# Mish as h·(1−2r): one multiply by h instead of two, a cap on exp(h), and a new instruction order

## The chip, the core and the metric

The kernel runs on one core of one Trainium2 chip. The metric is the device time of one execution in microseconds (us); lower is better. Three runs of the kernel before took 521.38, 521.48 and 521.93 us, a median of 521.48.

## The reference

Two stages follow each other. The first is a gated linear recurrence over 768 steps for 4 batches of 8 heads of width 48; the second is a feed-forward layer with the activation mish, over all 3072 tokens:

```python
f = 1.0 / (1.0 + np.exp(-f_logit))
for t in range(S):
    state = f[:, :, t, :, None] * state + np.einsum('bhd,bhe->bhde', k[:, :, t], v[:, :, t])
    y[:, :, t] = np.einsum('bhd,bhde->bhe', q[:, :, t], state)
...
h = x @ w_in                                   # 3072 x 384 times 384 x 2048
sp = np.where(h > 20.0, h, np.log1p(np.exp(np.minimum(h, 20.0))))
g = h * np.tanh(sp)
return (g @ w_out).astype(np.float32)          # 3072 x 2048 times 2048 x 384
```

With u = exp(h), tanh(log(1+u)) is n/(n+2) for n = u² + 2u, and that is also 1 − 2r for r = 1/((u+1)² + 1).

## The kernel before

**Recurrence.** The sequence is cut into 24 chunks of 128 steps (6 chunks times 4 batches). A chunk `n` goes through four steps, `attn0` to `attn3`. `load` and `prep` bring in `l`, `k`, `q`, `v` and scale `k` and `q` by decays: L386 caps the logits, L387 and L388 take exp and log, L391 (a matmul) or L396 (a scan) sums along the chunk, L403 and L404 take the exponentials, and L306 multiplies `k` and `q`. L427 forms the scores, L433 masks them into `a`. L452 transposes `k`, L455 copies it out, L470 forms the state update, L483 or L486 and L488 add it (`mid`, `tmp`), and L533 decays the state on GpSimd. L505 and L517 form the outputs; L543 to L550 split them into a high and a low part in `xt`, and L556 moves one quarter of `xt` by DMA to the place where the feed-forward wants it.

**Feed-forward.** Four chunks make a group of 512 tokens, and the hidden width is cut into 16 blocks of 128, so there are 6 × 16 = 96 units. For each unit L247 runs 9 matmuls into one of two PSUM tiles `h` (three slices of the model width, each as high·high, low·high and high·low products), `mish` turns `h` into `g`, then into `gh` (L264) and the rest `gl` (L265), and L270 runs 9 matmuls into three PSUM tiles `o`, two units behind (`LAG = 2`). A unit's L247 can only start when the mish of two units earlier has read its `h` for the last time, at L263. Weights come as 64-bit numbers and are split by `split_w` (L349 to L359) during the first 16 blocks.

**Mish before.** L257 and L258 on ScalarE give u with a cap at 10, L259 on VectorE gives n, L260 h·n, L261 and L262 on ScalarE 1/(n+2) as exp(−log(n+2)), L263 the product, L264 the high part, L265 on GpSimd the rest:

```python
("act", ..., lambda: nc.scalar.activation(u, h, AF.Relu, bias=hcap, scale=-1.0)),          # L257
("act", ..., lambda: nc.scalar.activation(u, u, AF.Exp, bias=hcap, scale=-1.0)),           # L258
("dve", ..., lambda: nc.vector.scalar_tensor_tensor(n, u, 2.0, u, ALU.add, ALU.mult)),     # L259
```

**Order.** All steps are collected in `Plan` with a cost each; `pack` lays them out on the engines, `SEEDS` names random changes of the ranking, and the kernel issues the instructions of every engine in the order of the planned starts. Each engine works through its own queue in that order. Until the first L270 the plan also puts filler matmuls (`idle`, L339, on a tile of zeros) where it expects the TensorE to have nothing to do. One filler in the program is two matmuls in the trace, as every matmul on plain f32.

Of the kernel before, what the change touches and what calls it, by code (L numbers as in the profile page):

```python
# [35 lines left out]
H_CAP = 10.0  # L36
# [11 lines left out]
]  # L48
NR = 3
LAG = 2  # L50

# [151 lines left out]
def recurrence_moe_kernel(  # L203
# [29 lines left out]
    two = ctile([P, 1], F32, "two")  # L233
    hcap = ctile([P, 1], F32, "hcap")
# [18 lines left out]
    def mish(h, n, g, gh, gl):  # L253

        u = n
        return (
            ("act", T_ACT(GT, True, 1), 0, lambda: nc.scalar.activation(u, h, AF.Relu, bias=hcap, scale=-1.0)),  # L257
            ("act", T_ACT(GT, False, 1), 0, lambda: nc.scalar.activation(u, u, AF.Exp, bias=hcap, scale=-1.0)),  # L258
            ("dve", T_DVE(GT), 1, lambda: nc.vector.scalar_tensor_tensor(n, u, 2.0, u, ALU.add, ALU.mult)),  # L259
            ("dve", T_DVE(GT), 0, lambda: nc.vector.tensor_tensor(g, h, n, ALU.mult)),  # L260
            ("act", T_ACT(GT, False, 1), 0, lambda: nc.scalar.activation(h, n, AF.Ln, bias=two)),  # L261
            ("act", T_ACT(GT, True), 0, lambda: nc.scalar.activation(h, h, AF.Exp, scale=-1.0)),  # L262
            ("dve", T_DVE(GT), 0, lambda: nc.vector.tensor_tensor(g, g, h, ALU.mult)),  # L263
            ("act", T_ACT(GT), 0, lambda: nc.scalar.activation(gh, g, AF.Copy)),  # L264
            ("pool", T_POOL(GT), 1, lambda: nc.gpsimd.tensor_tensor(gl, g, gh.bitcast(F32), ALU.subtract)),  # L265
        )
# [8 lines left out]
    with tc.tile_pool(name="work", bufs=1) as pool, tc.tile_pool(  # L275
# [33 lines left out]
        def consts():  # L309
# [6 lines left out]
            nc.gpsimd.memset(two, 2.0)  # L316
            nc.gpsimd.memset(hcap, H_CAP)
            nc.gpsimd.memset(ones, 1.0)

# [282 lines left out]
        def out_unit(u):  # L602
# [18 lines left out]
            if last:  # L621
                dst = halves[g] if j < NF - 1 else out[:, g * GT : (g + 1) * GT]
                for m in range(NK):
                    if part:
                        add("dve", T_DVE(GT), lambda m=m: nc.vector.tensor_tensor(ob_[m], o_[m], ob_[m], ALU.add),
# [190 lines left out]
```

## Time and profile before

| | |
|---|---|
| median of three runs | 521.48 us |
| span of the profiled execution, first to last instruction | 519.1 us |
| TensorE busy (matmul) | 505.9 us, 97% |
| ScalarE busy | 416.4 us, 80% |
| VectorE busy | 366.7 us, 71% |
| GpSimd busy | 156.1 us, 30% |
| first L247 starts | 45.29 us |
| last L270 group starts, 45 matmuls | 502.56 us |

The profiled execution has no time of its own beside its span; what lies around the span is taken as 521.48 − 519.1 = 2.4 us, the distance to the median. PE is the TensorE's matmuls, PEld its weight loads, ACT the ScalarE, DVE the VectorE, POOL the GpSimd, SP the queue that issues the DMAs. A busy PE is no proof of a PE at its best rate, because matmuls overlap and their ends are modelled; the distance between starts tells the rate.

### The profile page before, as it was taken

Reading aid. Unit: us, or ns where it says so; the run is one execution under the profiler, and the core shown is the slowest. Engines: PE = TensorE matmul, PEld = TensorE weight load, DVE = VectorE, ACT = ScalarE, POOL = GpSimd, SP = SyncE. Lnnn points to the kernel's source line nnn. Section 1 sums busy time; section 2 is a strip of 40 time slices with the busy share of each in tenths; the row PEclk is TensorE's granted clock in tenths of the full one; section 3 lists DMA queues with packets and bytes.
Section 4 is the critical chain, followed back from the end, with each engine's and each line's share of the span. In section 5 each row is a group of like instructions: output and inputs, shape, how many; then the busy total and the mean of one; then the engine's idle time right before and its main releaser. Section 6 shows DMA issues by size and latency. Waiting matters only on the chain.

```text
span 519.1 us, 12812 instructions
## 1 busy us (share of the span) xinstructions
PE 505.9 (97%) x5250; PEld 399.9 (77%) x5250; DVE 366.7 (71%) x592; ACT 416.4 (80%) x731; POOL 156.1 (30%) x134
## 2 busy tenths in 40 slices
PE   8799999999999999999999999999999999999995
PEld 6677777777787778778778778778787787878884
DVE  3679999999997876856767667665668564545451
ACT  6698988988999888888778788877778786777771
POOL 1142443333332223232233232323232221232322
PEclk9799999999999999999999999999999999999999
DMA  8977634524601533320213321130210000010001
GB/s 257 346 227 265 218 125 152 158 87 142 221 25 38 189 102 111 124 59 27 82 40 92 104 82 43 45 101 10 74 49 1 4 2 32 2 60 0 1 1 66
DMA packets 22625, 48.86 MB, mean 94 GB/s; under 512 B 2656, under 2 KB 3808, under 8 KB 22560
## 3 DMA queue, kind: packets, MB, share of 16 engines
q1 hardware_dynamic: 22560, 47.98, 28.2%
q8 instruction: 42, 0.69, 0.5%
q14 instruction: 23, 0.19, 0.1%
HBM read 39.32 MB, written 6.29 MB: 88 GB/s over the span
## 4 chain that ended last, share of the span: by engine, by line
PE 85%; DVE 5%; ACT 3%; DMA 2%; issue 2%; SPq 1%; POOL 0%; DVEq 0%; ACTq 0%
PE h L247 37%; PE o L270 36%; PE at L517 2%; PE at L505 2%; PE at L470 2%; PE at L427 2%; PE at L452 2%; DMA raw<-ww 1%; DMA l<-fl 1%; DVE wt L356 1%; SPq L368 1%; PE o L339 1%; DVE n L259 1%; DVE wt L354 1%; DVE g L263 1%
## 5 line engine op out<-in xcount | busy, mean ns | idle before, releaser
L265 POOL TENSOR_TENSOR gl<-g,gh 128x512 fp32r<-128x512 f32 x96 | 128.9, 1344 | 292.9 <-ACT gh L264 257.0
L247 PE MATMUL h<-xt,wh 128*128 128x512 f32 x576 | 185.0, 402 | 1.2 <-DVE g L263 1.2
L247 PEld LDWEIGHTS h<-xt,wh 128*128 128x128 f32 x576 | 105.2, 188 | 27.7 <-DVE g L263 2.9
L270 PE MATMUL o<-gh,wh 128*128 128x512 f32 x288 | 116.0, 403 | 0.0
L247 PE MATMUL h<-xt,wl 128*128 128x512 f32 x288 | 113.7, 395 | 0.0
L270 PE MATMUL o<-gh,wl 128*128 128x512 f32 x288 | 113.7, 395 | 0.0
L270 PE MATMUL o<-gl,wh 128*128 128x512 f32 x288 | 113.7, 395 | 0.0
L259 DVE SCALAR_TENSOR_TENSOR n<-n 128x512 f32<-128x512 f32 x96 | 67.9, 707 | 54.6 <-ACT n L258 54.2
L257 ACT ACTIVATE n<-h,hcap 128x512 f32<-128x512 f32 x96 | 65.7, 685 | 32.6 <-PE h L247 31.9
L263 DVE TENSOR_TENSOR g<-g,h 128x512 f32<-128x512 f32 x96 | 65.4, 682 | 36.8 <-ACT h L262 36.2
L261 ACT ACTIVATE h<-n,two 128x512 f32<-128x512 f32 x96 | 65.9, 686 | 18.6 <-DVE g L260 17.5
L264 ACT ACTIVATE gh<-g 128x512 fp32r<-128x512 f32 x96 | 60.1, 627 | 19.3 <-DVE g L263 14.1
L260 DVE TENSOR_TENSOR g<-h,n 128x512 f32<-128x512 f32 x96 | 66.2, 690 | 9.3 <-POOL gl L265 1.3
L258 ACT ACTIVATE n<-n,hcap 128x512 f32<-128x512 f32 x96 | 69.2, 721 | 2.3
L270 PEld LDWEIGHTS o<-gh,wh 128*128 128x128 f32 x288 | 54.0, 187 | 13.7 <-issue 0.3
L270 PEld LDWEIGHTS o<-gl,wh 128*128 128x128 f32 x288 | 54.0, 187 | 13.2
L247 PEld LDWEIGHTS h<-xt,wl 128*128 128x128 f32 x288 | 54.0, 187 | 13.2
L270 PEld LDWEIGHTS o<-gh,wl 128*128 128x128 f32 x288 | 54.1, 188 | 12.0
L262 ACT ACTIVATE h<-h 128x512 f32<-128x512 f32 x96 | 55.8, 582 | 1.7
L396 DVE TENSOR_TENSOR_SCAN cum<-go,l 128x512 f32<-128x512 f32 x20 | 26.9, 1343 | 0.9 <-ACT l L388 0.8
L433 DVE TENSOR_TENSOR a<-at,causal 128x256 f32<-128x256 f32 x44 | 17.6, 418 | 10.5 <-PE at L427 10.5
L533 POOL TENSOR_TENSOR state<-tmp,ends 128x256 f32<-128x256 f32 x20 | 16.0, 802 | 24.8 <-PE at L505 16.9
(103 smaller groups left out, 500.6 us busy)
## 6 DMA issues: line engine op xcount, KB each, us to landing
raw<-ww SPq DMA_DIRECT2D x16, 768.0 KB, 4.9
v<-vn SPq DMA_DIRECT2D x24, 256.0 KB, 3.7
k<-kk SPq DMA_DIRECT2D x23, 256.0 KB, 3.0
q<-qq SPq DMA_DIRECT2D x23, 256.0 KB, 3.7
l<-fl SPq DMA_DIRECT2D x20, 256.0 KB, 2.7
out<-ob SPq DMA_DIRECT2D x18, 256.0 KB, 2.9
xt<-xt SPq DMA_DIRECT2D x15, 128.0 KB, 2.1
half<-ob SPq DMA_DIRECT2D x6, 256.0 KB, 2.2
```

Source lines behind the costliest of these rows:

```text
L247: nc.tensor.matmul(h, w[:, j, a * P : (a + 1) * P], xt[:, x, a, :], start=(n == 0), stop=(n == 3 * NK - 1))
L257: ("act", T_ACT(GT, True, 1), 0, lambda: nc.scalar.activation(u, h, AF.Relu, bias=hcap, scale=-1.0)),
L258: ("act", T_ACT(GT, False, 1), 0, lambda: nc.scalar.activation(u, u, AF.Exp, bias=hcap, scale=-1.0)),
L259: ("dve", T_DVE(GT), 1, lambda: nc.vector.scalar_tensor_tensor(n, u, 2.0, u, ALU.add, ALU.mult)),
L260: ("dve", T_DVE(GT), 0, lambda: nc.vector.tensor_tensor(g, h, n, ALU.mult)),
L261: ("act", T_ACT(GT, False, 1), 0, lambda: nc.scalar.activation(h, n, AF.Ln, bias=two)),
L262: ("act", T_ACT(GT, True), 0, lambda: nc.scalar.activation(h, h, AF.Exp, scale=-1.0)),
L263: ("dve", T_DVE(GT), 0, lambda: nc.vector.tensor_tensor(g, g, h, ALU.mult)),
L264: ("act", T_ACT(GT), 0, lambda: nc.scalar.activation(gh, g, AF.Copy)),
L265: ("pool", T_POOL(GT), 1, lambda: nc.gpsimd.tensor_tensor(gl, g, gh.bitcast(F32), ALU.subtract)),
L270: nc.tensor.matmul(o, w[:, j, m * P : (m + 1) * P], x, start=(first and i == 0), stop=(last and i == 2))
L396: add("dve", 2 * T_DVE(w) - 70, lambda s=s, cum=cum: nc.vector.tensor_tensor_scan(cum.rearrange("p a c -> p (a c)"), go[:, s].rearrange("p ...
```

## The change

Mish is computed as −2·h·(r − ½) with r = 1/((u+1)² + 1), and the factor −2 is put into the copies that take `o` out of PSUM. There are eight operations instead of nine: exp on ScalarE straight from `h`, cap and +1 in one VectorE operation, a square on ScalarE, log and exp as before but written to `n` in SBUF, and one VectorE operation that subtracts ½ and multiplies by `h`. The cap is now exp(10) on u. The tile `half`, which holds ½, is made at the start by two small ScalarE operations; two memsets go. `SEEDS` is replaced by another list and the whole order is packed anew. Since lines move, L247 of before is L244 in the changed kernel, L257 and L258 become L258 (exp), L259 (cap and +1) and L255 (square); L261 to L265 keep their numbers and L260 is gone.

```diff
-H_CAP = 10.0
+U_CAP = 22026.46484375
 SEEDS = [
-    10000067, 10000086, ...
+    13000029, 13000046, ...
...
+        square = (
+            ("dve", T_DVE(GT), 1, lambda: nc.vector.tensor_tensor(n, n, n, ALU.mult)) if on_dve else
+            ("act", T_ACT(GT), 0, lambda: nc.scalar.activation(n, n, AF.Square))
+        )
         return (
-            ("act", T_ACT(GT, True, 1), 0, lambda: nc.scalar.activation(u, h, AF.Relu, bias=hcap, scale=-1.0)),
-            ("act", T_ACT(GT, False, 1), 0, lambda: nc.scalar.activation(u, u, AF.Exp, bias=hcap, scale=-1.0)),
-            ("dve", T_DVE(GT), 1, lambda: nc.vector.scalar_tensor_tensor(n, u, 2.0, u, ALU.add, ALU.mult)),
-            ("dve", T_DVE(GT), 0, lambda: nc.vector.tensor_tensor(g, h, n, ALU.mult)),
-            ("act", T_ACT(GT, False, 1), 0, lambda: nc.scalar.activation(h, n, AF.Ln, bias=two)),
-            ("act", T_ACT(GT, True), 0, lambda: nc.scalar.activation(h, h, AF.Exp, scale=-1.0)),
-            ("dve", T_DVE(GT), 0, lambda: nc.vector.tensor_tensor(g, g, h, ALU.mult)),
+            ("act", T_ACT(GT, True), 0, lambda: nc.scalar.activation(n, h, AF.Exp)),
+            ("dve", 70 + GT / 1.92, 1, lambda: nc.vector.tensor_scalar(n, n, U_CAP, 1.0, ALU.min, ALU.add)),
+            square,
+            ("act", T_ACT(GT, False, 1), 0, lambda: nc.scalar.activation(n, n, AF.Ln, bias=ones)),
+            ("act", T_ACT(GT), 0, lambda: nc.scalar.activation(n, n, AF.Exp, scale=-1.0)),
+            ("dve", T_DVE(GT), 0, lambda: nc.vector.scalar_tensor_tensor(g, n, half_, h, ALU.subtract, ALU.mult)),
             ("act", T_ACT(GT), 0, lambda: nc.scalar.activation(gh, g, AF.Copy)),
...
-            nc.gpsimd.memset(two, 2.0)
-            nc.gpsimd.memset(hcap, H_CAP)
             nc.gpsimd.memset(ones, 1.0)
+            nc.scalar.activation(half_, ones, AF.Ln, bias=ones)
+            nc.scalar.activation(half_, half_, AF.Exp, scale=-1.0)
...
-    nc.vector.tensor_tensor(ob_[m], o_[m], ob_[m], ALU.add)
+    nc.vector.scalar_tensor_tensor(ob_[m], o_[m], -2.0, ob_[m], ALU.mult, ALU.add)
-    nc.scalar.activation(ob_[m], o_[m], AF.Copy)
+    nc.scalar.activation(ob_[m], o_[m], AF.Copy, scale=-2.0)
-    nc.vector.tensor_copy(ob_[m], o_[m])
+    nc.vector.tensor_scalar(ob_[m], o_[m], -2.0, None, ALU.mult)
```

`SQ_DVE` is empty, so all 96 squares run on ScalarE. The three places at which the new order matters follow; a number behind a tile's name tells one buffer from another.

The TensorE where the feed-forward starts, in the kernel before: the transpose for the sixth chunk, three fillers, the first unit (`h_129`), then the update of the sixth chunk.

```order
L517 MATMUL at_127<-a_100,v_91 32x64
L452 MATMUL at_128<-ident,k_86 128x128 x4
L339 MATMUL o_133<-state_74 128x256 x3
L247 MATMUL h_129<-xt_107,wh 128x512 x2
L247 MATMUL h_129<-xt_107,wl 128x512
L247 MATMUL h_129<-xt_107,wh 128x512 x2
L247 MATMUL h_129<-xt_107,wl 128x512
L247 MATMUL h_129<-xt_107,wh 128x512 x2
L247 MATMUL h_129<-xt_107,wl 128x512
L470 MATMUL at_128<-v_92,kt_96 64x64 x2
```

The same place in the changed kernel:

```order
L517 MATMUL at_126<-a_99,v_90 32x64
L452 MATMUL at_127<-ident,k_85 128x128 x4
L244 MATMUL h_128<-xt_106,wh 128x512 x2
L244 MATMUL h_128<-xt_106,wl 128x512
L244 MATMUL h_128<-xt_106,wh 128x512 x2
L244 MATMUL h_128<-xt_106,wl 128x512
L244 MATMUL h_128<-xt_106,wh 128x512 x2
L244 MATMUL h_128<-xt_106,wl 128x512
L244 MATMUL h_129<-xt_106,wh 128x512 x2
L244 MATMUL h_129<-xt_106,wl 128x512
```

The three fillers ahead of the first unit are gone, and the second unit (`h_129`) follows the first with nothing in between. Over the whole program the TensorE has 21 fillers instead of 28: ahead of the first unit 18 instead of 25, and behind it three in each.

The TensorE a little later, in the kernel before: the last fillers, between the outputs of the sixth chunk and the third unit, which takes the `h` of the first.

```order
L517 MATMUL at_126<-a_101,v_92 32x64
L517 MATMUL at_127<-a_102,v_92 32x64
L339 MATMUL o_133<-state_74 128x256 x2
L247 MATMUL h_129<-xt_107,wh 128x512 x2
L247 MATMUL h_129<-xt_107,wl 128x512
```

In the changed kernel the last fillers stand behind the second unit, ahead of the update of the sixth chunk; its scores and then the third unit follow.

```order
L244 MATMUL h_129<-xt_106,wh 128x512 x2
L244 MATMUL h_129<-xt_106,wl 128x512
L339 MATMUL o_132<-state_73 128x256 x3
L470 MATMUL at_127<-v_91,kt_95 64x64 x2
L470 MATMUL at_126<-v_91,kt_95 64x64 x2
```

So in the changed kernel the third unit comes with less recurrence work ahead of it: the sixth chunk's outputs and the seventh's transpose, which lay between the second and the third unit, now come behind the third.

SP's queue where the first group's `xt` is moved, in the kernel before (`raw` is a block of weights, 768 KB):

```order
L556 DMA xt_107<-xt_107 32x2x384
L349 DMA raw_122<-ww 128x1536
L556 DMA xt_107<-xt_107 32x2x384 x2
L556 DMA xt_107<-xt_107 32x2x128 x3
L371 DMA v_90<-vn 128x512
```

And in the changed kernel:

```order
L368 DMA k_83<-kk 128x512
L368 DMA q_86<-qq 128x512
L556 DMA xt_106<-xt_106 32x2x384 x3
L556 DMA xt_106<-xt_106 32x2x128 x3
L349 DMA raw_121<-ww 128x1536
L371 DMA v_89<-vn 128x512
```

All six transfers of `xt` now go ahead of the block of weights instead of five behind it.

## Rows read from the trace of the kernel before

**Rows 1.** Busy time by 20 us stretches, two of them: bounds of the stretch, its length, then busy us and (instructions) of PE, PEld, DVE, ACT and POOL, the granted TensorE clock, the DMA engines' share, GB/s.

```profile
40.00:60.00 20.00, 19.03 (x310) 14.46 (x302) 20.00 (x33) 17.64 (x33) 6.16 (x5) 1.00 0.68 231
...
140.00:160.00 20.00, 20.00 (x87) 15.87 (x86) 18.03 (x27) 19.12 (x32) 6.08 (x5) 1.00 0.12 33
```

**Rows 2.** The chain of work that ended last, towards its end: start, length, what (the third row is the last group of matmuls).

```profile
456.36 4.20 PE h L247 x18
460.56 4.20 PE o L270 x18
...
502.56 10.52 PE o L270 x45
```

**Rows 3.** Waits of the TensorE in the whole span, those of the feed-forward: line <- what it waited for: us in total, times, longest.

```profile
PE h L247 <- DVE g L263: 1.2, 3, 0.6
```

**Rows 4.** The chain of work that ended last, from 16 to 30 us.

```profile
16.57 0.57 PE o L427 x23
17.14 2.01 issue
...
19.73 2.00 PE h L391 x8
...
23.91 0.85 PE o L339 x2
...
25.19 0.73 PE o L339 x2
25.93 0.89 PE at L391 x8
...
27.25 0.87 PE o L339 x4
...
28.75 1.06 PE o L339 x4
```

**Rows 5.** Busy time in one stretch of 1 us, columns as in rows 1.

```profile
24.00:25.00 1.00, 1.00 (x5) 0.82 (x5) 0.32 (x1) 0.64 (x2) 0.11 (x1) 0.50 0.65 141
```

**Rows 6.** The TensorE in order of time, the last correction matmul of the first group and the first unit: start, us, engine, line, operation, tiles, shapes, count; where there is a bracket, the idle time ahead of it and what ended it.

```profile
37.57 0.38 PE L546 MATMUL at<-xt,minus 128*128 128x256 f32 x1
...
45.29 0.82 PE L247 MATMUL h<-xt,wh 128*128 128x512 f32 x2
```

**Rows 7.** ScalarE's last operation on the first group's `xt` and SP's issues of its transfers, in order of time; then, from the list of DMA issues, two kinds of `xt` transfers: count, KB each, median us from issue to landing. The three of 32 KB are the last of the first group; the fifteen belong to the later groups.

```profile
37.99 0.39 ACT L548 ACTIVATE xt<-at 128x256 fp32r<-128x256 f32 x1
...
37.48 3.21 SPq L556 DMA_DIRECT2D xt<-xt  x5
...
xt<-xt SPq DMA_DIRECT2D x15, 128.0 KB, 2.1
...
xt<-xt SPq DMA_DIRECT2D x3, 32.0 KB, 4.2
```

**Rows 8.** The TensorE in order of time behind the second unit, columns as in rows 6.

```profile
50.97 0.59 PE L339 MATMUL o<-state 128*128 128x256 f32 x2
51.92 0.66 PE L452 MATMUL at<-ident,k 128*128 128x128 f32 x4 [0.36 <-POOL k L306]
...
53.92 1.13 PE L339 MATMUL o<-state 128*128 128x256 f32 x4
55.63 0.73 PE L247 MATMUL h<-xt,wh 128*128 128x512 f32 x2 [0.58 <-DVE g L263]
...
61.55 0.74 PE L247 MATMUL h<-xt,wh 128*128 128x512 f32 x2 [0.37 <-DVE g L263]
```

**Rows 9.** Groups by line and shape: line, engine, operation, out<-in, count, busy us, mean ns of one, idle time before and its releasers. First VectorE, then ScalarE; beside mish's own lines stand others (L386, L388, L404 and a narrow L306) whose form a new operation has or whose wait matters.

```profile
L259 DVE SCALAR_TENSOR_TENSOR n<-n 128x512 f32<-128x512 f32 x96 | 67.9, 707 | 54.6 <-ACT n L258 54.2
L260 DVE TENSOR_TENSOR g<-h,n 128x512 f32<-128x512 f32 x96 | 66.2, 690 | 9.3 <-POOL gl L265 1.3 <-DVE n L259 0.5
L263 DVE TENSOR_TENSOR g<-g,h 128x512 f32<-128x512 f32 x96 | 65.4, 682 | 36.8 <-ACT h L262 36.2
...
L386 DVE TENSOR_SCALAR l<-l 128x512 f32<-128x512 f32 x23 | 11.1, 488 | 1.0 <-DMA l<-ft 0.7 <-DMA l<-fl 0.2
...
L306 DVE TENSOR_TENSOR k<-k,inv 128x256 f32<-128x256 f32 x2 | 0.8, 422 | 3.8 <-DMA k<-kk 3.8
...
L258 ACT ACTIVATE n<-n,hcap 128x512 f32<-128x512 f32 x96 | 69.2, 721 | 2.3
L261 ACT ACTIVATE h<-n,two 128x512 f32<-128x512 f32 x96 | 65.9, 686 | 18.6 <-DVE g L260 17.5 <-DVE flag L600 1.0
L257 ACT ACTIVATE n<-h,hcap 128x512 f32<-128x512 f32 x96 | 65.7, 685 | 32.6 <-PE h L247 31.9
L264 ACT ACTIVATE gh<-g 128x512 fp32r<-128x512 f32 x96 | 60.1, 627 | 19.3 <-DVE g L263 14.1 <-PE o L270 3.8 <-PE h L247 0.8
L262 ACT ACTIVATE h<-h 128x512 f32<-128x512 f32 x96 | 55.8, 582 | 1.7
L388 ACT ACTIVATE l<-l,ones 128x512 f32<-128x512 f32 x23 | 16.5, 719 | 0.4
...
L404 ACT ACTIVATE at<-cum 128x512 f32<-128x512 f32 x20 | 11.8, 591 | 0.7 <-DVE xt L550 0.7
```

**Rows 10.** The last unit's mish, its first operation and its last on `h`, in order of time (ScalarE, then VectorE), columns as in rows 6.

```profile
502.59 0.69 ACT L257 ACTIVATE n<-h,hcap 128x512 f32<-128x512 f32 x1 [0.65 <-PE h L247]
...
507.42 0.69 DVE L263 TENSOR_TENSOR g<-g,h 128x512 f32<-128x512 f32 x1 [1.27 <-ACT h L262]
```

More of the change, by code (lines that the diff above doesn't have):

```diff
@@ L42 @@
 SEEDS = [
[5 rows of a table removed]
+    13000029, 13000046, 13000059, 13000123, 13000311, 13000334, 13000348, 13000585, 13000621, 13000645,
+    13000837, 13000891, 13002054, 13004137, 13004871, 13025036, 13026811, 13045422, 13050334, 13059718,
 ]
@@ L50 @@
 LAG = 2
+SQ_DVE = ()
 class Plan:
@@ L232, in recurrence_moe_kernel @@
     causal = ctile([P, CH], F32, "causal")
-    two = ctile([P, 1], F32, "two")
-    hcap = ctile([P, 1], F32, "hcap")
+    half_ = ctile([P, 1], F32, "half")
     ones = ctile([P, 1], F32, "ones")
@@ L250, in moe_in, with mish @@
                 n += 1
-    def mish(h, n, g, gh, gl):
-        u = n
-        return (
-            ("act", T_ACT(GT, True, 1), 0, lambda: nc.scalar.activation(u, h, AF.Relu, bias=hcap, scale=-1.0)),
-            ("act", T_ACT(GT, False, 1), 0, lambda: nc.scalar.activation(u, u, AF.Exp, bias=hcap, scale=-1.0)),
-            ("dve", T_DVE(GT), 1, lambda: nc.vector.scalar_tensor_tensor(n, u, 2.0, u, ALU.add, ALU.mult)),
-            ("dve", T_DVE(GT), 0, lambda: nc.vector.tensor_tensor(g, h, n, ALU.mult)),
-            ("act", T_ACT(GT, False, 1), 0, lambda: nc.scalar.activation(h, n, AF.Ln, bias=two)),
-            ("act", T_ACT(GT, True), 0, lambda: nc.scalar.activation(h, h, AF.Exp, scale=-1.0)),
-            ("dve", T_DVE(GT), 0, lambda: nc.vector.tensor_tensor(g, g, h, ALU.mult)),
+    def mish(h, n, g, gh, gl, on_dve=False):
+        square = (
+            ("dve", T_DVE(GT), 1, lambda: nc.vector.tensor_tensor(n, n, n, ALU.mult)) if on_dve else
+            ("act", T_ACT(GT), 0, lambda: nc.scalar.activation(n, n, AF.Square))
+        )
+        return (
+            ("act", T_ACT(GT, True), 0, lambda: nc.scalar.activation(n, h, AF.Exp)),
[4 more added lines that the diff above has]
+            ("dve", T_DVE(GT), 0, lambda: nc.vector.scalar_tensor_tensor(g, n, half_, h, ALU.subtract, ALU.mult)),
             ("act", T_ACT(GT), 0, lambda: nc.scalar.activation(gh, g, AF.Copy)),
@@ L624, in out_unit @@
                     if part:
-                        add("dve", T_DVE(GT), lambda m=m: nc.vector.tensor_tensor(ob_[m], o_[m], ob_[m], ALU.add),
+                        add("dve", T_DVE(GT), lambda m=m: nc.vector.scalar_tensor_tensor(
+                            ob_[m], o_[m], -2.0, ob_[m], ALU.mult, ALU.add),
                             [("o", m)], pairs(("ob", m)))
                     elif m == 1:
-                        add("act", T_ACT(GT, True), lambda m=m: nc.scalar.activation(ob_[m], o_[m], AF.Copy),
+                        add("act", T_ACT(GT, True), lambda m=m: nc.scalar.activation(ob_[m], o_[m], AF.Copy, scale=-2.0),
                             [("o", m)], pairs(("ob", m)))
                     else:
-                        add("dve", T_DVE(GT), lambda m=m: nc.vector.tensor_copy(ob_[m], o_[m]),
+                        add("dve", T_DVE(GT), lambda m=m: nc.vector.tensor_scalar(ob_[m], o_[m], -2.0, None, ALU.mult),
                             [("o", m)] + ["flag"] * (u == len(units) - 1), pairs(("ob", m)))
@@ L648, in recurrence_moe_kernel @@
                 kh, kn, kg = ("h", hs), ("n", us), ("g", us)
-                ops = mish(h, n_[us], g_[us], gh_[gs], gl_[gs])
+                ops = mish(h, n_[us], g_[us], gh_[gs], gl_[gs], u in SQ_DVE)
                 rw = (
-                    ([kh], [kn]), ([], [kn]), ([], [kn]), ([kh, kn], [kg]), ([kn], [kh]), ([], [kh]),
-                    ([kh], [kg]), ([kg], [("gh", gs)]), ([kg, ("gh", gs)], [("gl", gs)]),
+                    ([kh], [kn]), ([], [kn]), ([], [kn]), ([], [kn]), ([], [kn]),
+                    ([kh, kn], [kg]), ([kg], [("gh", gs)]), ([kg, ("gh", gs)], [("gl", gs)]),
                 )
@@ L744, in recurrence_moe_kernel @@
                         moe_out(o[m], m, gh, gl, 0, True, True, *(w[:, :, NK * P :] for w in wj))
-                        nc.vector.tensor_tensor(total_o[:, m], total_o[:, m], o[m], ALU.add)
+                        nc.vector.scalar_tensor_tensor(total_o[:, m], o[m], -2.0, total_o[:, m], ALU.mult, ALU.add)
                 nc.sync.dma_start(out.rearrange("(m p) t -> p m t", p=P)[:, :, tok], total_o)
```

5 rows, old and new, of the table SEEDS are left out of this document.

## The prediction

> **What bounds the kernel now.** I read the busy times first, then the end of the chain of waits, then the waits of the TensorE, and last the stretch before the feed-forward. From 140 to 160 us the TensorE is busy for all 20 us, while VectorE and ScalarE too are busy for 18.0 and 19.1 [rows 1]. Which of the three sets the pace is told by the distance between groups of matmuls: 18 of L247 take 4.20, 18 of L270 behind them 4.20, the last 45 take 10.52 [rows 2]. That is 0.233 us each throughout, with no gap. The 96 units have 96 × 18 = 1728 such matmuls, 403 us, and the change touches none of them. In the whole span L247 waited for mish (for L263, which gives `h` back) three times, for 1.2 us [rows 3]. So from some 62 us on the TensorE runs its queue without stops, and what VectorE saves there is worth nothing. Only the part before that can become shorter: 45.3 us until the first unit [rows 6], and 16 us of run-in behind it.
>
> In that part the reader is to see three things. First, in the chain from 16 to 30 us, a wait of 2.01 us called "issue" after 23 matmuls of a block of 32 [rows 4]: the TensorE waited for nothing the profile shows. After it the granted clock is 0.50 [rows 5], that is 1.2 instead of 2.4 GHz, and eight L391 take 2.00 us that take 0.89 a little later [rows 4]. Second, fillers lie on the chain itself: 0.85, 0.73, 0.87 and 1.06 us [rows 4]. They are cheap where the TensorE would stand anyway and cost their full time where it would not. Third, from the last L546 at 37.57 to the first unit at 45.29, 7.7 us, no idle time stands ahead of the first unit [rows 6]; and the run-in has fillers and three waits [rows 8].
>
> **VectorE and ScalarE per unit.** VectorE loses 0.707 + 0.690 + 0.682 = 2.08 us and gains a tensor-scalar in SBUF, as L386 at 0.488, and a two-operand operation that reads `h` in PSUM, as L260 at 0.690: 1.18 us [rows 9]. That is 0.90 less, 86 us over 96 units. ScalarE has 0.685 + 0.721 + 0.686 + 0.582 + 0.627 = 3.30 before. After, exp from PSUM is priced as L404 (0.591), square, exp and copy in SBUF as L264 (0.627 each), the log with its bias as L388 (0.719): 3.19, so 0.11 less [rows 9]. Both savings are hidden behind the TensorE after 62 us, so they count nothing in the sum. If that cover were gone, VectorE's would be the larger, see the rivals. What counts is the length of the way from `h` finished to `h` given back: before 0.685 + 0.721 + 0.707 + 0.690 + 0.686 + 0.582 + 0.682 = 4.75, after 0.591 + 0.488 + 0.627 + 0.719 + 0.627 + 0.690 = 3.74 [rows 9]. One microsecond less, wherever a unit waits for it.
>
> **The small edits.** The factor −2 in the copies changes neither engine, shape nor source: nothing, with VectorE's and ScalarE's idle time as cover, except for the last copies, whose tail I leave as it is. The two ScalarE operations for `half` come in the first 6 us. VectorE waits 3.8 us for the first `k` there [rows 9], which covers them; uncovered they would cost some tenths. The two memsets were on an idle engine.
>
> **Until the first unit.** The work on the TensorE ahead of it is the same, but there are 18 fillers in place of 25. One filler takes (0.87 + 1.06) / 4 = 0.48 us [rows 4]. Up to the block with the "issue" wait, six stand in place of seven, beside a wait for data that I leave unchanged. Counting matmuls in the order, the wait came at the 222nd, and in the new order the 222nd is in the same block of scores (198 come before it instead of 199). My estimate is that the same wait returns there.
>
> Behind that block and up to the last L546, nine fillers become five. Of those nine, six lie on the chain (two matmuls each [rows 4]); the other three stand beside work of ScalarE. Four fillers are 1.9 us. I take the chain's share of it, 6/9, 1.3 us; the ends are 0, if each removed filler only uncovers a wait, and 1.9. Behind the last L546 nine become seven, 1.0 us, with ends 0 and 1.0. Does the data allow that? The first unit needs `xt`: the last L548 ends at 38.4, SP needs 3.21 / 5 = 0.64 for each of three issues, and such a transfer lands after 4.2 us [rows 7]. That gives 44.5, so 0.8 of the 1.0 is free even without the change in SP's queue. In the new order the 768 KB of weights go behind all six transfers, and the later `xt` transfers landed after 2.1 us [rows 7], which leaves room. The weights are late by as much; they are the block of the fifth unit, which before came after the one at 61.55 [rows 8]. Together −2.3 us, between 0 and −2.9.
>
> **The run-in.** Before, three fillers (0.59 + 1.13) and three waits (0.36, 0.58, 0.37) stand behind the first unit [rows 8]: 3.0 us. After, there are again three fillers, and two of those waits, 0.95 us, were for L263, at the end of a way that is now 1.0 shorter. The third, for the seventh chunk's `k`, goes with its L452, which moves behind the fourth unit. Against it: the third unit now has less recurrence work ahead of it (one transpose and one block of outputs less), so `h` of the first must come back earlier. The TensorE has 4.2 us for two units, 1.5 for fillers and some 1.3 for update and scores; `h` is finished after 2.3. That leaves 4.7 us for a way of 3.74, with weight splitting in between on VectorE. Ends: all 1.3 us of waits gone, or a new wait that is 0.7 longer than these. I take −0.9, nearer to the first end, because the way is shorter than the room it has.
>
> **The remainder.** A block of outputs and a transpose that stood apart now stand together once; the tenths that this may save I take as −0.2, with 0 as the other end. The order behind 62 us has the same blocks of recurrence between the same matmuls. Sum: −2.3 − 0.9 − 0.2 = −3.4 us. The span of 519.1 becomes 515.7; with the 2.4 us around it, that is 518.1 against the median of 521.48.
>
> **Rivals.**
>
> *Fillers become waits.* The planner put fewer fillers because it expects fewer pauses, but ScalarE and the transfers may hold the TensorE at the same times. For it: ScalarE works for 17.6 of 20 us from 40 to 60 [rows 1], and a third of the nine fillers cost nothing. Against: six lie on the chain. Then only a few tenths remain: 521.2.
>
> *The instruction wait changes.* If it is absent, 2.01 us and the half clock go: L391 alone gains 1.1 of 2.00 [rows 4], the other work until the clock is back about as much, some 4 us in all: 514.1. If it is longer, or a second one comes, as much is lost: 522.1, minus what waits for data hide, about 521.5. The removed fillers speak for the latter, since they were matmuls as well. The Trainium skill (TensorE: Matmul & The Clock Gate, What's actually happening) says that "the default state is throttled, and activity releases the throttle"; by that rule removing fillers is a risk, and the sum would be 521.5 instead of 518.1. The trace agrees as far as one fall goes: 0.50 after a stand of 2 us [rows 4, 5].
>
> *`h` comes back late (slower).* The new mish goes to ScalarE three times in a row behind VectorE's first operation, and ScalarE is busy for 19.1 of 20 us from 140 to 160 [rows 1]. Units come at 8.4 us for two [rows 2], 2.1 of them L247 itself, so `h` must be back within 6.3 us. The last unit, with no recurrence around it, took from 502.59 to 508.11, 5.5 us, for a bare 4.75 [rows 10, 9]. From 6.3 us on each unit waits for the excess. If that were 0.25 us in the units until 160 us, some 25 (115 us at 4.2 would be 27, less for the recurrence), it would cost 6.2: 524.3. Against: the bare way is 3.74, and ScalarE's load falls. The Trainium skill (ScalarE: Activation LUTs, Rules for kernel authors) wants multiplications on VectorE, not ScalarE; by it the squares belong on the other engine, and the sum with them on a full ScalarE would be 524.3. The trace doesn't bear it out for this form: a two-tensor f32 multiply takes 0.682 on VectorE, a copy on ScalarE 0.627 [rows 9].
>
> *VectorE was the bound.* It is busy for 20.0 of 20 us from 40 to 60 [rows 1]. If it set the pace of the first 16 units, 16 × 0.90 = 14 us would go: 507. Against: the TensorE is busy for 19.0 there, and waited for L263 only 1.2 us.
>
> **How the numbers follow.** The forecast has a chance of 0.60, fillers become waits 0.14, the instruction wait gone 0.09, longer 0.06, `h` late 0.08, VectorE the bound 0.03. A measurement of this kernel can tell about 0.2%, 1.0 us, from no change, so faster means below 520.4 and slower above 522.5. Faster: 0.60 + 0.09 + 0.03 = 0.72. Same: 0.14 and half of 0.06, 0.17. Slower: 0.08 and the other half, 0.11. The forecast's own range, from the ends of its terms, is 521.48 − 4.4 to 521.48 + 0.7; most of it lies between 517 and 520. The range given goes from 515.0 to 521.8: it takes in the forecast, the first rival and part of the second, and leaves out late `h`, VectorE as the bound and most of the case without the instruction wait, together under 0.2.
>
> **What would show it.** Right: the first L244 starts at about 43, the third unit with a wait under 0.5; behind 62 us rows of 4.20 as before; VectorE near 280 us busy, ScalarE near 406; a wait named "issue" near 17 us and the clock at 0.50 behind it. Wrong: first unit at 45 or later with idle time ahead of L470, L505 or L546 (first rival); no half clock, or a second stretch of it; waits for L263 summing to several microseconds after 62 us (third).

## The result, and the profile after

The changed kernel takes 509.42 us (median; 509.08 to 510.63) against 521.43 beside it: 0.9772 of it, 95% interval 0.9750 to 0.9794. The forecast was 518.1 and the range ended at 515.0: the direction was right, the size was not.

In the profiled executions the span falls by 11.6 us, from 519.1 to 507.5. I divide both at two points: the first unit's start, and the start of the last 45 matmuls. The chain of waits of the changed kernel ends like this (start, length, what):

```profile
478.64 4.08 PE h L244 x18
482.72 4.08 PE o L270 x18
486.80 4.08 PE h L244 x18
491.00 10.46 PE o L270 x45
```

Against [rows 2] each group of 18 takes 4.08 instead of 4.20, on the same operands in the same shape. From the first unit to the last 45 matmuls there are 451.0 us (491.00 − 39.97) instead of 457.3 (502.56 − 45.29), and 16.5 behind it in both. So 5.3 us are gained ahead of the first unit, and 6.2 in the stretch behind it, most of which I had called untouched.

The TensorE in order of time, changed kernel (start, us, line, tiles, shapes, count; in brackets the idle time ahead and what ended it):

```profile
16.75 0.69 PE L427 MATMUL o<-q,k 64*64 64x64 f32 x32 [0.59 <-DVE q L306]
...
25.78 0.62 PE L427 MATMUL at<-q,k 64*64 64x64 f32 x25
27.55 0.34 PE L427 MATMUL at<-q,k 64*64 64x64 f32 x7 [1.16 <-issue]
...
39.97 0.47 PE L244 MATMUL h<-xt,wh 128*128 128x512 f32 x1
...
47.22 0.73 PE L244 MATMUL h<-xt,wh 128*128 128x512 f32 x2 [0.43 <-DVE g L263]
...
56.15 0.74 PE L244 MATMUL h<-xt,wh 128*128 128x512 f32 x2 [0.57 <-DVE g L263]
...
63.15 0.73 PE L244 MATMUL h<-xt,wh 128*128 128x512 f32 x2 [1.30 <-DVE g L263]
...
105.51 0.73 PE L244 MATMUL h<-xt,wh 128*128 128x512 f32 x2 [0.98 <-DVE g L263]
```

The block that stood for 2.01 us after 23 matmuls [rows 4] runs through; a wait named "issue" comes one block of scores later and takes 1.16. Behind the first unit four units wait for `h`, three before [rows 3]. The waits in sum (us, times, longest), and two stretches with the columns of rows 1:

```profile
PE h L244 <- DVE g L263: 3.3, 4, 1.3
PE at L427 <- issue: 1.2, 1, 1.2
```

```profile
24.00:25.00 1.00, 0.82 (x57) 0.75 (x64) 1.00 (x3) 1.00 (x4) 0.17 (x1) 1.00 1.03 367
...
140.00:160.00 20.00, 20.00 (x88) 16.16 (x87) 9.23 (x14) 17.19 (x32) 6.48 (x5) 1.00 0.00 1
```

The clock is 1.00 where it was 0.50 [rows 5]. From 140 to 160 us VectorE is busy for 9.23 us instead of 18.03 [rows 1], and TensorE for 20.00 in both: what VectorE saves there buys nothing, as forecast. The new mish by groups, to be held against [rows 9]:

```profile
L263 DVE SCALAR_TENSOR_TENSOR g<-n,half,h 128x512 f32<-128x512 f32 x96 | 71.5, 745 | 105.5 <-ACT n L262 103.8 <-POOL gl L265 1.4
L261 ACT ACTIVATE n<-n,ones 128x512 f32<-128x512 f32 x96 | 69.2, 721 | 2.2
L262 ACT ACTIVATE n<-n 128x512 f32<-128x512 f32 x96 | 60.4, 629 | 2.3
L255 ACT ACTIVATE n<-n 128x512 f32<-128x512 f32 x96 | 60.2, 627 | 23.9 <-DVE n L259 23.7
...
L258 ACT ACTIVATE n<-h 128x512 f32<-128x512 f32 x96 | 56.5, 589 | 20.8 <-PE h L244 20.5
L259 DVE TENSOR_SCALAR n<-n 128x512 f32<-128x512 f32 x96 | 50.8, 529 | 43.4 <-ACT n L258 43.2
```

The way from `h` finished to `h` given back is 0.589 + 0.529 + 0.627 + 0.721 + 0.629 + 0.745 = 3.84 us; I had 3.74. The last operation is dearer (0.745 for 0.690), the first one of VectorE too (0.529 for 0.488).

### The profile page after: what moved, and what is told of

It reads as the page before. It is cut to its first block, busy times and chain, and to the rows that moved or that the text cites. A ratio compares the mean times of both kernels' runs of the same rounds, so it can differ in the third digit from the quotient of the medians.

```text
span 507.5 us, 12552 instructions
## 1 busy us (share of the span) xinstructions
PE 490.7 (97%) x5236; PEld 393.2 (77%) x5236; DVE 296.1 (58%) x496; ACT 404.4 (80%) x733; POOL 152.8 (30%) x132
## 4 chain that ended last, share of the span: by engine, by line
PE 84%; DVE 7%; ACT 4%; DMA 2%; issue 2%; DVEq 0%; SPq 0%; ACTq 0%
PE o L270 38%; PE h L244 36%; PE at L517 2%; PE at L505 2%; PE at L470 2%; PE at L427 2%; PE at L452 2%; DVE wt L354 1%; DMA raw<-ww 1%; DVE g L263 1%; DVE wt L356 1%; DMA q<-qq 1%; DVE cum L396 1%; DVE wt L353 1%; DVE n L259 1%
## 5 line engine op out<-in xcount | busy, mean ns | idle before, releaser
L265 POOL TENSOR_TENSOR gl<-g,gh 128x512 fp32r<-128x512 f32 x96 | 127.2, 1325 | 307.5 <-ACT gh L264 294.7
L244 PE MATMUL h<-xt,wh 128*128 128x512 f32 x576 | 179.9, 393 | 3.4 <-DVE g L263 3.3
L263 DVE SCALAR_TENSOR_TENSOR g<-n,half,h 128x512 f32<-128x512 f32 x96 | 71.5, 745 | 105.5 <-ACT n L262 103.8
L244 PEld LDWEIGHTS h<-xt,wh 128*128 128x128 f32 x576 | 106.3, 188 | 29.2 <-DVE g L263 7.0
L270 PE MATMUL o<-gh,wh 128*128 128x512 f32 x288 | 117.2, 407 | 0.0
L270 PE MATMUL o<-gl,wh 128*128 128x512 f32 x288 | 112.7, 391 | 0.0
L244 PE MATMUL h<-xt,wl 128*128 128x512 f32 x288 | 112.4, 390 | 0.0
L270 PE MATMUL o<-gh,wl 128*128 128x512 f32 x288 | 112.3, 390 | 0.0
L255 ACT ACTIVATE n<-n 128x512 f32<-128x512 f32 x96 | 60.2, 627 | 23.9 <-DVE n L259 23.7
L259 DVE TENSOR_SCALAR n<-n 128x512 f32<-128x512 f32 x96 | 50.8, 529 | 43.4 <-ACT n L258 43.2
L258 ACT ACTIVATE n<-h 128x512 f32<-128x512 f32 x96 | 56.5, 589 | 20.8 <-PE h L244 20.5
L261 ACT ACTIVATE n<-n,ones 128x512 f32<-128x512 f32 x96 | 69.2, 721 | 2.2
L270 PEld LDWEIGHTS o<-gl,wh 128*128 128x128 f32 x288 | 54.0, 188 | 12.2 <-POOL gl L265 0.2
L270 PEld LDWEIGHTS o<-gh,wh 128*128 128x128 f32 x288 | 54.0, 188 | 12.0
L244 PEld LDWEIGHTS h<-xt,wl 128*128 128x128 f32 x288 | 54.1, 188 | 11.7
L262 ACT ACTIVATE n<-n 128x512 f32<-128x512 f32 x96 | 60.4, 629 | 2.3
L270 PEld LDWEIGHTS o<-gh,wl 128*128 128x128 f32 x288 | 54.2, 188 | 9.9
L550 DVE TENSOR_TENSOR xt<-at,xt 128x256 fp32r<-128x256 f32 x40 | 16.5, 419 | 15.2 <-ACT xt L543 15.2
L396 DVE TENSOR_TENSOR_SCAN cum<-go,l 128x512 f32<-128x512 f32 x20 | 25.4, 1269 | 0.0
L470 PEld LDWEIGHTS at<-v,kt 64*64 64x64 f32 x704 | 13.3, 134 | 8.6 <-issue 2.8
```

The source lines that it names most:

```text
L244: nc.tensor.matmul(h, w[:, j, a * P : (a + 1) * P], xt[:, x, a, :], start=(n == 0), stop=(n == 3 * NK - 1))
L255: ("act", T_ACT(GT), 0, lambda: nc.scalar.activation(n, n, AF.Square))
L258: ("act", T_ACT(GT, True), 0, lambda: nc.scalar.activation(n, h, AF.Exp)),
L259: ("dve", 70 + GT / 1.92, 1, lambda: nc.vector.tensor_scalar(n, n, U_CAP, 1.0, ALU.min, ALU.add)),
L262: ("act", T_ACT(GT), 0, lambda: nc.scalar.activation(n, n, AF.Exp, scale=-1.0)),
L263: ("dve", T_DVE(GT), 0, lambda: nc.vector.scalar_tensor_tensor(g, n, half_, h, ALU.subtract, ALU.mult)),
```

## Experiments

**First question: why do the long matmuls follow each other faster?** The first theory comes from the tiles' addresses. The change drops one of three [P,1] constants, each takes 32 bytes, and so every tile behind them stands 32 bytes lower (`xt` at 151168 instead of 151200); the weights stand ahead of them and stay at 384. "S" is the time from the first unit to the last 45 matmuls in the profiled run.

Run 1, the changed kernel with the 32 bytes back:

```diff
+    pad = ctile([P, 1], F32, "pad")
     ones = ctile([P, 1], F32, "ones")
```

> The changed kernel with one more [P,1] constant tile, so that xt, gh, gl and all tiles behind it stand 32 bytes higher, at the addresses of the kernel before (xt0 151200, that is 32 beyond a multiple of 64). Theory A, the place of the streamed operand in SBUF sets the distance of the long matmuls: 18 of L244 take 4.20 again instead of 4.08, everything else as in the changed kernel, first unit at 40.0; 1728 matmuls by 5 ns more: about 518 us against 509.4. Theory B, the new order of the work or the new mish (other traffic of ScalarE and VectorE on SBUF and PSUM) sets it: 4.08 stays, 509.4 us. Theory C, another cause on the early stretch moves with the addresses too: the first unit at 45.

Run 2, the kernel before without them:

```diff
-    two = ctile([P, 1], F32, "two")
-    hcap = ctile([P, 1], F32, "hcap")
+    both = ctile([P, 2], F32, "both")
+    two, hcap = both[:, 0:1], both[:, 1:2]
```

> The kernel before with its two [P,1] constants (two, hcap) as the columns of one tile, so that all later tiles stand 32 bytes lower, at the addresses of the changed kernel (xt0 151168, a multiple of 64). Operations, order and waits are those of before. Theory A (place in SBUF): 18 of L247 take 4.08, and 9 us go from 521.4: about 512.5 us, with the first unit at 45.3, the issue wait and the half clock as before. Theory B (order or mish): 4.20 and 521.4 us.

The chain of waits near the end, run 1, then run 2:

```profile
485.83 4.20 PE h L245 x18
490.04 4.20 PE o L271 x18
```

```profile
484.36 4.08 PE h L247 x18
488.44 4.08 PE o L270 x18
```

Both came out as theory A said, with some 7 us where it had 9. Run 1: 517.13 us, S 457.8 against 451.0; run 2: 514.97, 0.9852 (0.9802 to 0.9901) of the kernel before beside it, S 450.3 against 457.3, its first unit still at 46.3. So the 32 bytes are worth some 7 us in either kernel, and the new order and mish together gain nothing there.

Two runs asked which place it is. Run 3 has a pad of 64 bytes (`[P, 16]`), run 4 a `[P, 1]` tile in the work pool ahead of `gh`:

> The changed kernel with a [P,16] tile more: all later tiles stand 64 bytes higher (xt0 151232). Theory A in the form that only the offset within 64 bytes counts: 4.08 and 509.4 us, as the changed kernel. If the offset within 128 bytes counts, or any move of the tiles disturbs it: 4.20 and about 518 us. Theory B: 509.4 us too, so this run alone does not tell A from B.

> The changed kernel with a [P,1] tile between g and gh in the work pool: xt stays at a multiple of 64, gh, gl (the streamed operands of L270) and ob stand 32 beyond one. Theory A: 18 of L244 keep 4.08, 18 of L270 take 4.20; 864 matmuls by 5 ns more, about 513.5 us. If what ScalarE and VectorE read and write beside it were what counts, or the weights: 4.08 for both and 509.4 us; if one misplaced tile slows all: 518 us.

Run 3: 513.0 us, groups of 18 in 4.12, neither of the two values. Run 4: 514.6 us, S 455.6; L270's matmuls, whose streamed tile moved, come 233.3 ns apart on average, L244's 230.5. L244 has its short distance too, but only after a run-in: of the last 18 in a row, the first five distances are 228 to 236 ns and all others 226 or 227, and most of its runs have nine matmuls. Why there is a run-in behind the slower matmuls, no run shows. Offsets within 64 bytes don't explain run 3. Run 5, 128 bytes (`[P, 32]`), was to settle it:

> The changed kernel with a [P,32] tile more: all later tiles 128 bytes higher (xt0 151296). If the offset within 128 bytes sets the distance of the long matmuls (32 gave 232 to 233 ns, 64 gave 229, 0 gave 227 to 228): 227 to 228 and 509.5 to 510.5 us, as the changed kernel. If the 229 ns of the run with 64 bytes came from that chip: 227 to 229 as well, and then 64 and 128 stand alike. If any shift costs: 229 or more, 513 us.

It took 516.58 us, at 232.6 and 232.5 ns: a multiple of 128, and bad. The theory of alignment alone had fallen. The next one: the place of the streamed tile relative to the weights, which are loaded while it streams (weight loads busy for 393.2 us beside 490.7 us of matmuls in the changed kernel). Run 6 moves everything, run 7 the weights and the constants next to them, run 8 is another distance (`[P, 64]`):

```diff
+    pad = ctile([P, 1], F32, "pad")
     wh = ctile([P, NF, W_TILE], F32R, "wh")
```

> The changed kernel with a [P,1] tile ahead of the weights: wh, wl and all other tiles stand 32 bytes higher (wh 416, xt0 151200, gh0 192160). Theory D, the place of the streamed tile itself counts: 232 to 233 ns and 516.5 to 517.5 us, as with 32 bytes behind the weights. Theory R, the place of the streamed tile relative to the weights that are loaded beside it counts: 227 to 228.5 ns and 509.5 to 510.5 us.

```diff
+    pad = ctile([P, 1], F32, "pad")
     wh = ctile([P, NF, W_TILE], F32R, "wh")
...
-    half_ = ctile([P, 1], F32, "half")
-    ones = ctile([P, 1], F32, "ones")
+    both = ctile([P, 2], F32, "both")
+    half_, ones = both[:, 0:1], both[:, 1:2]
```

> The changed kernel with wh and wl 32 bytes higher (wh 416), and half and ones as the columns of one tile, so that xt, gh and gl stay where they are (xt0 151168, gh0 192128). Theory D (place of the streamed tile): 227 to 228.5 ns, 509.5 to 510.5 us. Theory R (place relative to the weights): another distance, by the runs so far 229 to 233 ns and 512 to 517 us. If the place of the weights itself counts: 232 here and in the run that moves all.

> The changed kernel with 256 bytes more ahead of the tiles behind the weights (xt0 151424). If the pattern comes back after 256 bytes: 227 to 228.5 ns and 509.5 to 510.5 us. If only some places are good: 229 to 233 ns and 513 to 517 us.

The chain near the end, run 6 (all moved), then run 7 (weights moved):

```profile
479.04 4.08 PE h L245 x18
483.12 4.08 PE o L271 x18
```

```profile
481.13 4.20 PE o L271 x18
485.33 4.20 PE h L245 x18
```

Run 6 has the streamed tile at the very address of the kernel before, and its groups take 4.08 (511.7 us, S 451.0); run 7 has it at the address of the changed kernel, and they take 4.20 (517.21, S 457.8). Run 8 is like run 6 (510.13, S 451.1). It is the distance between the two that counts. The last two fill the map, with pads of `[P, 24]` and `[P, 48]`, one execution each:

> The changed kernel with 96 bytes more behind the weights (xt0 151264, 150880 bytes beyond wh, 96 modulo 256). If only multiples of 256 are good and multiples of 64 a little better than the rest: 232 to 233 ns, 516 to 518 us. If the distance falls off with the way to the nearest multiple of 64: 231 to 233 as well. A better place: under 227 and 509 or less.

> The changed kernel with 192 bytes more behind the weights (xt0 151360, 192 modulo 256). If multiples of 64 are alike but for 128: 229 ns and 512 to 514 us, as with 64 bytes. If only multiples of 256 are good: 232 to 233 ns, 516 to 518 us. If it hangs on the sign: between these.

The table has means from the records of each trace: from start to start of two matmuls of one line that follow each other, distances over 300 ns left out. The last column takes only a stretch near the end of the last 45 matmuls in which ScalarE, VectorE and GpSimd are idle (four to ten distances).

| distance xt0 − wh, modulo 256 | kernels | ns from matmul to matmul, into `h` / into `o` | into `o`, the others idle | S, us |
|---|---|---|---|---|
| 0 | changed; runs 2, 6, 8 | 227.7 to 228.3 / 227.7 to 228.5 | 226.7 to 226.8 | 450.3 to 451.1 |
| 32 | before; run 1 | 233.3; 233.4 / 233.3; 233.1 | 233.6; 233.5 | 457.3; 457.8 |
| 64 | run 3 | 229.2 / 229.7 | 229.2 | 452.8 |
| 96 | run 9 | 233.1 / 233.1 | 233.8 | 457.9 |
| 128 | run 5 | 232.6 / 232.5 | 233.4 | 457.0 |
| 192 | run 10 | 233.4 / 233.3 | 233.3 | 458.0 |
| 224 | run 7 | 233.3 / 233.0 | 233.3 | 457.8 |

The last column answers the nearest rival. In the runs of the table the tiles that ScalarE, VectorE and GpSimd read and write stand as far from the weights as `xt` does, modulo 256, so their traffic could have been the cause. But the distances are the same while those three stand still: 226.7 ns from 497.7 to 500.1 us in the changed kernel, 233.3 from 504.7 to 507.4 in run 7.

The Trainium skill (SBUF — State Buffer, Who interferes with whom) gives TensorE two read ports, one for the moving operand and one for the weights, and calls them independent. These runs don't bear that out for time: between the changed kernel and run 7 the weights moved against the streamed tile, and 226.7 ns became 233.3 with no other compute engine at work. That the pattern comes back after 256 bytes rests on run 8 alone. Why 256 bytes, and why 64 is nearly as good, no run shows.

**Second question: where did the issue wait and the half clock go?** The page of the changed kernel lists an instruction queue of its own among the DMA queues (packets, MB, share of the 16 engines):

```profile
q8 instruction: 41, 0.67, 0.6%
```

Its packets are 16 KB each. The 0.67 MB are some 64 bytes for each of TensorE's 10,472 matmuls and weight loads, so I take the queue for TensorE's. Packets and waits of TensorE, from the records of each trace:

| kernel | packet from – to | TensorE goes on | stood | clock after it |
|---|---|---|---|---|
| before | 16.72 – 17.84 | 19.15 | 2.01 | 0.50 |
| changed | 14.59 – 15.68 | (did not stand) | 0 | 1.00 |
| changed, a later packet | 25.12 – 26.08 | 27.55 | 1.16 | 1.00 |
| run 1 | 15.98 – 17.04 | 18.34 | 0.61 | 1.00 |
| run 3 | 16.12 – 17.12 | 18.53 | 1.09 | 1.00 |

TensorE goes on 1.3 to 1.5 us after the packet's end in each row with a stand. The DMA engines were full around these packets: share 1.00 to 1.10 from 16 to 19 us before, 1.03 from 24 to 25 us above. The Trainium skill (Runtime: NRT & Kernel Launch, Instruction fetch mechanics) describes such a fetch, blocks of 256 instructions through a DMA queue of the sequencer's own, and calls the cost "mostly hidden". The trace agrees on the packets; of the cost, up to 2.71 us (run 12) and 2.99 us (run 17) were not hidden.

Run 11 moves the second weight block on SP of the kernel before behind the next four transfers; run 12 is the changed kernel once more; run 13 moves its fourth weight block in the same way.

```diff
-        for i in self.order():
+        order = self.order()
+        sp = [i for i in order if self.steps[i][0] == "sp"]
+        order.remove(sp[14])
+        order.insert(order.index(sp[18]) + 1, sp[14])
+        for i in order:
```

> The kernel before with one transfer moved: the second weight block of 768 KB is issued after the next four transfers on SP (k, l, v, q) instead of ahead of them. Theory Q: TensorE stands 2.0 us at L427 because its instructions come through the same DMA engines, behind data that were issued earlier (the packet of the instruction queue starts at 16.7 us, and TensorE goes on 2.4 us after such a start in each trace so far); with 768 KB less in front, the packet starts near 15, the wait is under 0.7 us and the granted clock stays 1.00; 3 to 4 us go up to the first unit, less what ScalarE then waits for the weights (L351 at 17.75, data some 2 us later): first unit at 42 to 44, 518 to 520 us. Rival, the wait is set by TensorE's own place in its instructions: 2.0 us at the same matmul, half clock, 45.3 and 521.5 or more.

> The changed kernel itself once more, on the chip of the three others and as their measure: 509.4 us if chips do not differ, 511 to 513 if the 3 us between it and the run with all tiles 64 bytes higher was a matter of the chip and not of those 64 bytes. First unit at 40 to 41, long matmuls at 227 to 229 ns.

> The changed kernel with one transfer moved: the fourth weight block of 768 KB goes on SP behind the next four transfers (q, l, v, k) instead of ahead of them. Theory Q (TensorE's instructions wait behind data in the DMA engines): the third packet of its instruction queue, which started at 25.1 to 28.0 us and let TensorE stand for 0.7 to 2.7, starts at 25 or before, the wait at the second L427 is under 1.0 in the profiled run, the granted clock stays 1.00, first unit at 39 to 41: 508 to 510 us, and no run at 514. Rival, that wait does not hang on this transfer: waits of 0.7 to 2.7 as before, and 509.5 to 514.

TensorE in run 11, then in run 12:

```profile
17.36 0.38 PE L431 MATMUL o<-q,k 64*64 64x64 f32 x9 [0.18 <-issue]
...
43.63 0.81 PE L251 MATMUL h<-xt,wh 128*128 128x512 f32 x2
```

```profile
17.80 0.34 PE L427 MATMUL o<-q,k 64*64 64x64 f32 x8 [0.57 <-issue]
...
30.30 0.49 PE L427 MATMUL at<-q,k 64*64 64x64 f32 x7 [2.71 <-issue]
```

and a stretch of 1 us behind that wait in run 12 (columns of rows 1):

```profile
32.00:33.00 1.00, 1.00 (x33) 0.92 (x32) 0.45 (x1) 1.00 (x2) 0.00 (x0) 0.50 0.70 213
```

The profiled execution of run 11 is as theory Q had it: packet at 14.89 (16.72 to 17.34 in the three traces of the old order without that move), 0.18 us at the same matmul, no half clock, first unit at 43.6 instead of 45.3. So data that go ahead of the instructions can make this wait; one trace shows it. Over ten executions the time does not change: 521.61 us, 0.9990 to 1.0036 of the kernel before, and the profiled one, 519.33, is the shortest of the ten. Part of the gain goes into a new wait of 1.2 us of TensorE for ScalarE, which now gets its weights 1.6 us late.

Run 12 shows what one profile hides. The same program has the 2.71 us wait and the half clock in its profiled execution, first unit at 44.59, 514.03 us, and 509.68 to 510.66 in the four others. S is 451.0 in both traces of this kernel, so its two profiles differ ahead of the first unit alone. Of nine executions of the changed kernel it is the only one above 510.7: those 4 us are lost seldom, not never. Run 13 gained nothing: packet at 25.45, 1.04 us, 510.56 us; that transfer is not what holds this packet. Why it started at 27.95 in run 12 and at 25.12 in the first trace, no run shows: while TensorE stood there, from 27 to 29 us, the DMA engines were not full (share 0.88 and 0.71).

**Third question: what are mish and order worth by themselves?** Run 14 puts the new mish into the steps of the old order, run 15 the old mish into the steps of the new one (addresses of the changed kernel in both, the queues of TensorE and SP unchanged). In run 14 square and log share a step and two steps stay empty. The core of run 15, shortened:

```diff
-("act", ..., lambda: nc.scalar.activation(n, h, AF.Exp)),
-("dve", ..., lambda: nc.vector.tensor_scalar(n, n, U_CAP, 1.0, ALU.min, ALU.add)),
+("act", ..., lambda: [relu(n, h), exp(n, n)]),
+("dve", ..., lambda: [scalar_tensor_tensor(n, n, 2.0, n, add, mult), tensor_tensor(h, h, n, mult)]),
```

> The kernel before with its order of TensorE and of the transfers as it is, but the new mish in the steps of the old one, the factor -2 in the copies, and tiles at the addresses of the changed kernel (xt0 151168). To be compared with the kernel before moved by 32 bytes (515.0 us). Issue wait of 2 us, half clock and first unit at 45.3 to 46.3 as before, long matmuls at 227 ns in every theory. Theory A: the waits for h in the run-in shrink from 2.6 us (of the moved kernel before) to under 1: about 513.5. Theory B, mish is covered by TensorE: 515. Rival, the three ScalarE operations in a row come back late in this order, which was made for the other way: 516 or more.

> The changed kernel with its order of TensorE, its transfers and its addresses, but the operations of the old mish in its steps: relu and exp, then the two-tensor operation and the product (written back into h, so that g is free as long as in the changed kernel), log and exp in n, the last product into g; copies without the factor. Against the changed kernel (509.4 and 510.5 in two sets of runs). Theory A, the shorter way pays in the run-in: the waits of L244 for h, 3.3 us in four units, grow by about 1.0 us per unit that waits, 4 us or more: 514 or above. Theory B, those waits come from the weight preparation ahead of mish on VectorE and not from the length of the way: within 1 us of the changed kernel. Theory C, VectorE sets the pace of the first 16 units: up to 14 us more, 524.

Waits of TensorE, run 14, then run 15:

```profile
PE h L247 <- DVE g L264: 8.3, 15, 1.1
```

```profile
PE h L246 <- DVE g L269: 33.8, 32, 2.8
```

Run 14 took 523.49 us, S 458.8, against 514.97 and 450.3 for the old mish in that order (run 2): the shorter way in an order made for the other one is slower. Run 15 took 568.35, far beyond every theory: 33.8 us of waits for `h`, and the clock fell to 0.50 five times. By my estimate these make up 39 of the 58 us by which S is longer (33.8 − 3.3, and half of five stretches of 3.4 us); the rest stays open. (A first form wrote the product into `g`, which steps of an earlier unit still had to read; it took 570.17 us and is not used.) Mish and order can't be priced apart; only the pair can. The pair, with the place of the tiles equal, is worth nothing in S: run 1 against before +0.5, the changed kernel against run 2 +0.7.

Why did the run-in not gain? In the chain of waits of the changed kernel, from 59 to 63 us:

```profile
59.57 1.21 DVE cum L396
60.78 0.45 DVE wt L353
61.24 0.23 DVE wl L359
61.47 0.55 issue
62.03 0.41 DVE n L259
62.44 0.67 DVE g L263
63.11 0.04 issue
63.15 2.35 PE h L244 x9
```

The chain lies on VectorE: the weight preparation (L353, L359) stands ahead of mish's first operation there. Run 16 leaves out three operations of the preparation from the third block on (the first of them is shown); run 17 leaves all in and lets mish pass the preparation on VectorE and ScalarE.

```diff
-add("dve", 469, lambda: nc.vector.tensor_scalar(t, t, 3, ...
+add("dve", 469, lambda: j < 2 and nc.vector.tensor_scalar(t, t, 3, ...
```

> The changed kernel without the three VectorE operations that put the bits of the weights together (0.55, 0.95 and 0.95 us), from the third block of weights on; loads, ScalarE's two operations and the last difference stay. It leaves out that part of the computation. Theory B (the weight preparation on VectorE ahead of mish makes the run-in wait): the waits of L244 for h in the four units of 47 to 106 us, 3.3 us, fall under 1.0; with them 2 to 3 us of the time: 507 to 508. Theory A' (ScalarE or the way itself): waits of 2.5 to 3.3 us and 509 to 510 stay.

> The changed kernel with the same operations, transfers and TensorE order; on VectorE and ScalarE the operations of mish go ahead of those of the weight preparation (up to 1.2 us of planned time) wherever both stand next to each other. Theory B (the preparation on VectorE ahead of mish makes the run-in wait): the waits of L244 for h, 3.3 us in four units, fall to 1 or 2; 1 to 2.5 us of the time go: 507.5 to 509. Theory A' (the way itself or ScalarE): 3.3 us stay and 509.5 to 510.5. Rival, the weights come late instead: waits of long matmuls for wl, 511 or more.

Run 16: 506.01 us, S 446.7 instead of 451.0; no wait for `h` is left in the list. So 4.3 us of S hang on VectorE's load by the preparation, 3.3 of them the waits for `h`. Run 17 took 518.80 us; the waits for `h` rose to 7.1 us in seven units, one "issue" wait of 3.0 came on top, and the clock fell to 0.50 twice (from 32.6 and from 121.3 us). Its theory fell. A reading that no run shows: passing the preparation puts it off and does not make it less, so units further on wait longer. What the best place for it is, stays open.

## Why the prediction was wrong

- **Failed step: "1728 such matmuls, 403 us, and the change touches none of them", and with it "behind 62 us rows of 4.20 as before".** The rows were read rightly, 0.233 us each, but the distance was taken as a property of the instruction. It was one of the place of its two operands, and the constant that the change drops moved one of them. Worth some 7 us (runs 1, 2, 6, 7): most of what is missing between −3.4 and −12.0. Run 1, the change without those 32 bytes, took 517.13 us, inside the range.
- **Until the first unit**: −2.3 forecast, −5.3 in this trace. The step that the same wait returns at the 222nd matmul was right about the place: in runs 1, 3 and 12 TensorE stands in that block after 24 matmuls. It was wrong about the length: in the sixteen traces with the new order the stand there is between nothing and 1.09 us, and each has a further one, of 0.47 to 2.99 us, one block of scores later. I had no cause for the wait; the packet table gives one. The half clock stayed away ahead of the first unit in twelve of the sixteen, so the rival with a chance of 0.09 was right about the clock, and about the wait only in part. The fillers' term is not shown by itself. With a half clock in both, the first unit moves from 45.3 to 44.6 (run 12, with "issue" waits 1.0 us longer in all). But TensorE's other pauses of 0.15 us and more ahead of the first unit grew too, from 3.0 to 6.1 us in the changed kernel and to 3.8 in run 12; 0.67 and 0.69 ahead of L452 and 0.45 ahead of L470 are among them. So some of the removed fillers became waits, as the first rival said; by this account the rest of the gain is the "issue" wait and its clock, but no run separates the two.
- **The small edits**: the two operations for `half` were put at nothing, covered by VectorE's wait for `k`. The chain of the changed kernel has both, and TensorE's first L391, the recurrence's first sum, starts at 5.25 us instead of 4.87, of which some 0.3 can be theirs. So they were not covered; what of it reaches the first unit, no run shows:

```profile
4.42 0.29 ACT half L317
...
5.11 0.09 ACT half L318
```

- **Run-in and remainder**: −1.1 forecast, +0.5 to +0.7 measured at equal places, from the first unit on. The third unit's wait is under 0.5 as forecast, but the later ones are longer. I had set the room of 4.7 us against a bare way of 3.74 and only mentioned the weight splitting between; run 16 prices three of its operations at 4.3 us over S. Here the rival with VectorE as the bound (0.03) was right in kind, for the first units only; the 14 us that it promised did not come, since the preparation fills VectorE there.
- **Behind 62 us** VectorE's saving bought nothing, as said. Its busy time ended at 296.1 us, not 280: 9 of the 16 us are the two dearer operations above, and most of the rest is that busy time counts operations that overlap once (one by one they fall by 77.0 us, the busy time by 70.6). ScalarE's ended at 404.4 (406 forecast). The tail stayed at 16.5 us from the last 45 matmuls on.
- **`h` late** came about only in small with this pair of order and mish: two of the four waits, 1.30 and 0.98 us, stand behind 62 us, where the prediction had none, and run 16, without part of the weight preparation, has neither. Runs 14 and 15 show what it costs when it comes in many units.

## What to carry to other kernels

A distance between matmuls that a trace shows everywhere is still not a constant: look at where the two operands stand, and when a tile is added, dropped or resized, compare the addresses behind it before calling the stream untouched. Price a change of operations together with the order made for it. And look at several times before trusting a profile's first stretch: one trace of the changed kernel had a 2.7 us stand that most of its executions had not.

## What was not expected of the hardware

- 128x512 matmuls from SBUF came 227.7 to 228.5 ns apart on average (226.7 with the other engines idle) where the streamed tile stood a multiple of 256 bytes from the weights, 229.2 to 229.7 at 64 beyond such a multiple, and 232.5 to 233.8 at 32, 96, 128, 192 and 224.
- TensorE's instructions arrive in 16 KB packets through the same DMA engines as the data; in the packet table it went on 1.3 to 1.5 us after a packet's end, after stands of up to 2.01 us (2.71 in run 12).
- Behind stands of 2.01 and 2.71 us the granted clock went to 0.50, the 1.2 GHz level; behind the stands of 0.18 to 1.16 us in the tables and rows here it stayed at 1.00. Two stands of 1.34 us at the same matmul went either way: 0.50 behind it in run 9, 1.00 in run 16.
